# A decayed attention followed by a gated MLP on one core: bias placed in PSUM, decays moved to k, more transposes by DMA, and a new order of all engines

## The chip, the cores and the metric

The kernel runs on one core of one Trainium2 chip. The metric is the device time of one execution in microseconds (us). Engines are named as in the profile: PE is the matrix engine (PEld its weight load), DVE the vector engine, ACT the scalar engine, POOL the GpSimd engine, SP the engine whose queue issues most DMAs.

## The reference

Inputs are q, k and v of 4 batches, 8 heads, 768 tokens and 64 elements per head, and one decay per head. Attention has no softmax: a token attends to earlier tokens with a weight that decays with distance, and the reference computes it in blocks of 64 with a running state.

```
intra = einsum('bhic,bhjc->bhij', qb, kb) * Dmask      # lam ** (i - j) for i >= j
intra = einsum('bhij,bhjd->bhid', intra, vb)
inter = einsum('bhid,bhde->bhie', qb * lam_pow, kv_state)
kv_state = lam_block * kv_state + einsum('bhsd,bhse->bhde', kb * rev_pow, vb)
x = (intra + inter) as (batch, token, 512)
h = relu(x @ w_in)                        # 512 -> 1024
u, v = h[..., :512], h[..., 512:]
v_n = (v - mean(v)) / sqrt(var(v) + 1e-6)
v_s = einsum('ts,bsd->btd', w_spatial, v_n) + b_spatial[None, :, None]
out = (u * v_s) @ w_out                   # 512 -> 512
```

`w_spatial` is 768 x 768 and mixes tokens, so the second half of a batch can start only when all tokens of the batch have their normalised v.

## The kernel before, in words

**Steps and batches.** Work is cut into 12 steps of 256 tokens of all heads; steps 0 to 2 are batch 0, steps 3 to 5 batch 1, and so on. Within a step 256 tokens are two chunks of 128. Each partition holds two adjacent tokens, so a "row" of the DMA is 512 bytes.

**Names of the work.** Everything is written out by hand in one string, `ORDER`. A token such as `SC.5.1.2.T` is a function (`SC`, line 322), its numbers, and the engine whose queue it goes into: T is PE, D is DVE, A is ACT, P is POOL, S is SP. Each engine runs its own tokens in the order of the string; between engines only data dependences and buffers order them. So a token that waits holds up all later tokens of its engine.

For a step n:

- `LK`, `LQ`, `LV` (line 184) load 512 KB of k, q, v; 3 buffers each (`NIN`).
- `KC`, `QC` cast k and q to bf16. `VD` (line 292) multiplies v by the decay of its token and casts, on POOL. `QM` (line 277) multiplies q by its decay, `EQ` (line 313) does so on the transposed q.
- `TK`, `TQ` (line 300) transpose by 8 products with the identity on PE, and `EK`, `EQ` copy the result out of PSUM to `kT`, `qT`. For steps 8 to 11 `DK`, `DQ` (lines 283, 287) transpose by DMA from SP's queue instead.
- `SC` (line 329) makes scores, `MK` (line 333) masks them into `a_sb`; `KV` (line 345) adds to the state in PSUM bank 7, `SS` copies the state out; `AV` (lines 366, 375) makes the attention's output, `EX` copies it to `xT`.
- `PV` (line 401) and `PU` (line 439) are the two halves of `x @ w_in`; `EV`, `EU` (lines 406, 408) apply relu on the way out of PSUM. `BN`, `RA`, `RD`, `VN` (lines 416 to 430) normalise v.

For a batch: `PW.b.f.i` (line 461) is the product with `w_spatial`, 6 products of 384 columns; `GB` (line 466, DVE) adds the bias from PSUM to the f32 tile `vsb`; `GM` (line 472, mostly POOL) multiplies by u into `gT`; `PO` (line 478) is the last product, `EO` copies out, `ST` stores 256 KB. `WT` (line 451) transposes `w_spatial` once on PE. The two adjacent tokens of a partition make the token order of x differ from the natural one; `WT` and `GM` undo it with strided views.

```
    def g_b(e, bb, f, i, b):
        nc.vector.tensor_tensor(out=vsb[...], in0=bank(b)[:, 0:HW], in1=bsp[...], op=ALU.add)
    def g_m(e, bb, f, i):
        vec(e).tensor_tensor(out=gT[...] "p (a y m) -> p a y m", in0=vsb[...],
                             in1=uT[...] "p (a m y) -> p a y m", op=ALU.mult)
```

PSUM has 8 banks; banks 0 to 6 are handed out by the last numbers of the tokens, and a token that needs a bank waits for the last reader of it. `GT` (line 235) is a tiny POOL copy that reads a loaded tile; it stands before the weight loads `WI`, `WS`, `WO`, which POOL issues with a cast to bf16, so that these start after that tile has landed.

Of the kernel before, what the change touches and what calls it, by code (L numbers as in the profile page):

```python
# [16 lines left out]
LK.0.2.S lam.A msk.P LQ.0.2.S LK.1.2.S idn.P mkc.D LV.0.2.S LB.6.T pos.P LN.6.A LK.2.2.S LL.D KC.0.2.P LX.A  # L17
LQ.1.2.S TK.0.6.T LT.0.A QC.0.2.D LQ.2.2.S TQ.0.5.T EK.0.6.A EQ.0.5.D KC.1.2.A SC.0.0.0.T LV.1.2.S SC.0.1.2.T
LT.2.A MK.0.0.0.D TK.1.6.T VD.0.2.P EK.1.6.A MK.0.1.2.D LV.2.2.S LT.1.A AV.0.0.0.T LK.3.2.S KV.0.0.T SS.0.0.A
GT.1.1.P WI.0.P QC.1.2.D KV.0.1.T AV.0.1.0.T KC.2.2.A LQ.3.2.S GT.1.1.P WI.1.P TQ.1.6.T EX.0.1.1.A TK.2.5.T  # L20
EQ.1.6.D GT.1.2.P WS.1.P EX.0.0.0.A QC.2.2.D EK.2.5.A SC.1.0.2.T LQ.4.2.S GT.1.2.P WS.0.P SC.1.1.0.T
MK.1.0.2.D TQ.2.6.T SS.0.1.A VD.1.2.P EQ.2.6.D MK.1.1.0.D SC.2.0.2.T SC.2.1.4.T MK.2.0.2.D AV.1.0.0.T KV.1.0.T
LV.3.2.S MK.2.1.4.D SS.1.0.A KV.1.1.T VD.2.2.P AV.1.1.0.T SS.1.1.A PV.0.0.6.T EX.1.1.1.A EX.1.0.0.A PV.0.1.1.T
EV.0.0.6.A AV.2.0.2.T BN.0.0.D PV.1.1.6.T EV.0.1.1.D KV.2.0.T BN.0.1.D PV.1.0.5.T SS.2.0.A EV.1.1.6.D RA.0.A
AV.2.1.2.T BN.1.1.D PU.1.0.6.T BS.S EV.1.0.5.A RD.0.D PU.0.1.4.T VN.0.0.D EX.2.1.3.A KC.3.2.P BN.1.0.D
EX.2.0.2.A PU.1.1.5.T EU.0.1.4.A EU.1.0.6.D PV.2.0.3.T RA.1.A VN.0.1.D EU.1.1.5.A RD.1.D TK.3.6.T VN.1.1.D
EV.2.0.3.A PU.2.0.2.T VN.1.0.D EK.3.6.A BN.2.0.D PV.2.1.3.T EU.2.0.2.A PU.2.1.6.T EV.2.1.3.A LK.4.2.S WT.3.2.T
BN.2.1.D EU.2.1.6.A QC.3.2.P WT.4.3.T WT.0.5.T EW.3.2.D RA.2.A WT.1.6.T LK.5.2.S EW.4.3.D EW.0.5.A WT.5.4.T
WT.2.2.T RD.2.D VN.2.1.D EW.5.4.A TQ.3.3.T QC.4.2.P VN.2.0.D PU.0.0.5.T EW.2.2.A EQ.3.3.D LQ.6.2.S EW.1.6.A
TQ.4.4.T VD.3.2.P SC.3.1.0.T EU.0.0.5.A EQ.4.4.D SC.3.0.2.T PW.0.0.1.6.T LQ.5.2.S MK.3.1.0.D PW.0.1.1.5.T  # L30
GB.0.0.1.6.D LV.4.2.S MK.3.0.2.D PW.0.1.0.4.T GM.0.0.1.P KC.4.2.A PW.0.0.0.6.T GB.0.1.1.5.D GB.0.1.0.4.D
LK.6.2.S GM.0.1.1.P TK.4.5.T GB.0.0.0.6.D PW.0.2.1.4.T GM.0.1.0.P EK.4.5.D LK.7.2.S AV.3.0.0.T GT.0.5.P WO.P
GB.0.2.1.4.D SC.4.0.2.T SC.4.1.5.T KV.3.0.T MK.4.0.2.D PW.0.3.1.4.T GM.0.2.1.P SS.3.0.A LV.6.2.S QC.6.2.P
MK.4.1.5.D KV.3.1.T AV.3.1.0.T KC.5.2.A PW.0.3.0.3.T GM.0.0.0.P SS.3.1.D GB.0.3.1.4.D LV.5.2.S QC.5.2.A
TK.5.6.T EX.3.1.1.D GM.0.3.1.P PW.0.2.0.2.T GB.0.3.0.3.D EX.3.0.0.A VD.4.2.P EK.5.6.A GM.0.3.0.D TQ.5.3.T
GB.0.2.0.2.D PV.3.1.5.T EQ.5.3.D PU.3.0.6.T EV.3.1.5.A GM.0.2.0.P AV.4.0.0.T BN.3.1.D EU.3.0.6.A SC.5.1.2.T
SC.5.0.4.T LQ.8.2.S KV.4.0.T MK.5.1.2.D PV.3.0.6.T SS.4.0.A MK.5.0.4.D KV.4.1.T EV.3.0.6.A AV.4.1.0.T LK.8.2.S
KC.6.2.P PO.0.0.3.T EX.4.0.0.A BN.3.0.D EX.4.1.1.A PO.0.1.6.T EO.0.0.3.D RA.3.A LK.9.2.S PV.4.0.2.T RD.3.D
SS.4.1.D EO.0.1.6.A VN.3.1.D VD.6.2.P VN.3.0.D PV.4.1.3.T EV.4.0.2.A ST.0.0.S TK.6.6.T BN.4.0.D EV.4.1.3.A
PO.0.2.2.T EK.6.6.A BN.4.1.D VD.5.2.P TQ.6.3.T LV.9.2.S EO.0.2.2.A PU.3.1.5.T EQ.6.3.D RA.4.A PO.0.3.6.T  # L40
# [24 lines left out]
EU.9.0.6.A AV.10.1.0.T MK.11.1.4.D PW.2.0.1.3.T EX.10.1.1.A SS.10.1.D PW.2.2.0.6.T GM.2.3.0.D GB.2.0.1.3.D
AV.11.0.4.T EX.10.0.0.D GM.2.0.1.P GB.2.2.0.6.D KV.11.0.T PV.10.0.3.T SS.11.0.D GM.2.2.0.P VN.9.0.D
AV.11.1.4.T EV.10.0.3.A PW.2.2.1.6.T EX.11.1.5.A BN.10.0.D EX.11.0.4.A PO.2.1.5.T GB.2.2.1.6.D PO.2.2.4.T
GM.2.2.1.P EO.2.1.5.D PU.11.1.6.T ST.2.1.S EO.2.2.4.A PO.2.4.5.T ST.2.2.S EU.11.1.6.A PV.11.1.4.T PV.11.0.6.T
EV.11.1.4.A PV.10.1.3.T BN.11.1.D EV.11.0.6.A PO.2.3.2.T BN.11.0.D EV.10.1.3.A PU.11.0.6.T BN.10.1.D RA.11.A
EO.2.3.2.A PU.10.1.3.T RD.11.D RA.10.A ST.2.3.S VN.11.1.D EU.11.0.6.A RD.10.D VN.11.0.D PO.2.5.2.T EU.10.1.3.A  # L70
VN.10.0.D VN.10.1.D PU.10.0.6.T EO.2.5.2.A PW.3.1.1.3.T ST.2.5.S EU.10.0.6.D PO.2.0.2.T GB.3.1.1.3.D
PW.3.0.0.6.T GM.3.1.1.P EO.2.0.2.A ST.2.0.S PW.3.1.0.4.T GB.3.0.0.6.D GM.3.0.0.P PW.3.0.1.6.T GB.3.1.0.4.D
GM.3.1.0.P PW.3.2.0.4.T EO.2.4.5.A GB.3.0.1.6.D ST.2.4.S GM.3.0.1.D PW.3.3.0.6.T GB.3.2.0.4.D PW.3.2.1.5.T
GM.3.2.0.P GB.3.3.0.6.D GM.3.3.0.D PW.3.3.1.6.T GB.3.2.1.5.D PO.3.0.4.T GM.3.2.1.P GB.3.3.1.6.D PO.3.1.5.T
GM.3.3.1.P EO.3.0.4.A PO.3.2.6.T ST.3.0.S EO.3.1.5.A PO.3.3.4.T ST.3.1.S EO.3.2.6.A PO.3.4.5.T ST.3.2.S
EO.3.3.4.A PO.3.5.6.T ST.3.3.S EO.3.4.5.A ST.3.4.S EH.3.5.6.0.A EH.3.5.6.1.D SH.3.5.0.A SH.3.5.1.S
"""


@with_exitstack  # L80
def kernel(
    ctx: ExitStack,
    tc: tile.TileContext,
    q: bass.AP,
    k: bass.AP,
    v: bass.AP,
    lam: bass.AP,
    moe_w_in: bass.AP,
# [11 lines left out]
    NT = S // P  # L100
    NCH = DM // P
    NR = S // (2 * P)
    T2 = 2 * P
    Q64 = 64
    MID = S // 2
    NIN, NCA, NTR, NA, NX, NO, NVS = 3, 2, 2, 2, 3, 4, 2

    const = ctx.enter_context(tc.tile_pool(name="const", bufs=1))
    psum = ctx.enter_context(tc.tile_pool(name="psum", bufs=1, space=bass.MemoryType.PSUM))

    def sb(shape, dt, name):
        return const.tile(shape, dt, name=name)
# [422 lines left out]
```

## Time and profile before

| what | before |
|---|---|
| device time, median of 3 runs | 152.93 us (152.09 to 153.16) |
| span of the profiled execution, first to last instruction | 151.2 us |
| median less that span | 1.7 us |
| PE busy | 133.6 us, 88% of the span |
| DVE busy | 106.9 us, 71% |
| ACT busy | 81.4 us, 54% |
| POOL busy | 75.6 us, 50% |
| moved by DMA | 30.73 MB, 203 GB/s on average |

How to read it: all numbers of engines and of the trace are of one profiled execution, whose own record is the span; the time of a run is a little longer than its span, and the last rows of the table put the two side by side. Busy PE is not PE at its peak, since the ends of pipelined products are modelled: in the chain of waits eight 256-column products stand at 0.87 us, while one of them alone is listed with 273 ns. Below, "row" is a group of instructions of one line and shape, "slice" is one fortieth of the span (3.78 us), and the DMA share is the mean busy share of the 16 DMA engines (it reaches 1.4 in places).

### The profile page before, as it was taken

Reading aid. Unit: us, or ns where it says so; the run is one execution under the profiler, and the core shown is the slowest. Engines: PE = TensorE matmul, PEld = TensorE weight load, DVE = VectorE, ACT = ScalarE, POOL = GpSimd, SP = SyncE. Lnnn points to the kernel's source line nnn. Section 1 sums busy time; section 2 is a strip of 40 time slices with the busy share of each in tenths; the row PEclk is TensorE's granted clock in tenths of the full one; section 3 lists DMA queues with packets and bytes.
Section 4 is the critical chain, followed back from the end, with each engine's and each line's share of the span. In section 5 each row is a group of like instructions: output and inputs, shape, how many; then the busy total and the mean of one; then the engine's idle time right before and its main releaser. Section 6 shows DMA issues by size and latency. Waiting matters only on the chain.

```text
span 151.2 us, 4756 instructions
## 1 busy us (share of the span) xinstructions
PE 133.6 (88%) x2026; PEld 87.2 (58%) x2026; DVE 106.9 (71%) x190; ACT 81.4 (54%) x146; POOL 75.6 (50%) x74
## 2 busy tenths in 40 slices
PE   1274947999999989977999999999999999999990
PEld 1264844677766754645766756556657655666540
DVE  1454593986999998685747799999958981936701
ACT  3987815698623837737724434765553344831161
POOL 7425980203669922780039975990293240016520
PEclk9999999999999999999999999999999999999999
DMA  3999999999988998999999799994170003121255
GB/s 108 300 290 290 283 216 216 217 248 304 281 221 237 172 301 216 269 310 342 319 341 276 142 306 311 202 208 177 41 138 4 2 4 139 57 81 72 74 219 197
DMA packets 52040, 30.73 MB, mean 203 GB/s; under 512 B 9522, under 2 KB 48946, under 8 KB 52018
## 3 DMA queue, kind: packets, MB, share of 16 engines
q1 hardware_dynamic: 49488, 27.53, 71.0%
q0 software_dynamic: 2384, 2.75, 10.6%
q8 instruction: 16, 0.26, 0.7%
q10 hardware_dynamic: 146, 0.13, 0.3%
q14 instruction: 6, 0.05, 0.1%
HBM read 24.77 MB, written 6.29 MB: 205 GB/s over the span
## 4 chain that ended last, share of the span: by engine, by line
PE 70%; DMA 16%; DVE 5%; SPq 4%; issue 2%; POOL 0%; ACT 0%; ACTq 0%
PE ps L461 20%; PE ps L439 13%; PE ps L401 13%; PE ps L478 11%; DMA q_in<-in_q_dram 10%; DMA win_sb<-in_moe_w_in_dram 6%; SPq L184 4%; PE ps L375 3%; PE ps L345 3%; PE ps L329 3%; PE ps L300 2%; PE ps L366 2%; PE ps L451 1%; DVE vsb L466 1%; DVE vn L430 1%
## 5 line engine op out<-in xcount | busy, mean ns | idle before, releaser
L472 POOL TENSOR_TENSOR gT<-vsb,uT 128x384 bf16<-128x384 f32 x27 | 30.1, 1128 | 33.6 <-DVE vsb L466 33.3
L461 PE MATMUL ps<-wt_sb,vn 128*128 128x384 bf16 x192 | 33.9, 327 | 0.0
L292 POOL TENSOR_TENSOR vd<-v_in,lv 128x1024 bf16<-128x1024 f32 x12 | 22.8, 1905 | 17.1 <-issue 6.4
L333 DVE TENSOR_TENSOR a_sb<-ps,m 128x1024 bf16<-128x1024 f32 x24 | 28.4, 1214 | 1.8 <-PE ps L329 1.6
L416 DVE BATCH_NORM_STATS2 st<-vh 128x6 f32<-128x512 bf16 x24 | 16.5, 688 | 11.9 <-ACT vh L406 11.7
L461 PEld LDWEIGHTS <-vn 128*128 128x128 bf16 x192 | 17.9, 98 | 11.9
L401 PE MATMUL ps<-win_sb,xT 128*128 128x512 bf16 x96 | 23.6, 380 | 0.8 <-DMA win_sb<-in_moe_w_in_dram 0.8
L439 PE MATMUL ps<-xT,win_sb 128*128 128x256 bf16 x192 | 24.1, 273 | 0.0
L478 PE MATMUL ps<-wout_sb,gT 128*128 128x512 bf16 x96 | 23.4, 380 | 0.0
L466 DVE TENSOR_TENSOR vsb<-ps,bsp 128x384 f32<-128x384 f32 x32 | 17.6, 552 | 6.8 <-PE ps L461 5.4
L439 PEld LDWEIGHTS <-win_sb 128*128 128x128 bf16 x192 | 18.3, 98 | 4.4
L168 ACT ACTIVATE o_sb<-ps 128x512 f32<-128x512 f32 (+1 forms) x21 | 12.3, 586 | 14.9 <-PE ps L478 10.7
L406 ACT ACTIVATE vh<-ps 128x512 bf16<-128x512 f32 x21 | 12.5, 597 | 13.6 <-PE ps L401 13.6
L406 ACT ACTIVATE uT<-ps 128x512 bf16<-128x512 f32 x22 | 13.2, 598 | 6.9 <-PE ps L439 6.7
L401 PEld LDWEIGHTS <-xT 128*128 128x128 bf16 x96 | 8.8, 98 | 9.6 <-issue 0.8
L478 PEld LDWEIGHTS <-gT 128*128 128x128 bf16 x96 | 9.0, 98 | 8.8
L168 ACT ACTIVATE s_sb<-ps 128x256 bf16<-128x256 f32 x14 | 5.3, 381 | 16.1 <-PE ps L345 16.1
L430 DVE TENSOR_SCALAR vn<-vh,mv,rstd 128x512 bf16<-128x512 bf16 x24 | 12.5, 551 | 0.3
L375 PE MATMUL ps<-a_sb,vd 64*64 64x128 bf16 x384 | 11.1, 225 | 1.7 <-DVE a_sb L333 1.0
L168 ACT ACTIVATE kc<-k_in 128x1024 bf16<-128x1024 f32 x7 | 7.4, 1056 | 8.4 <-PE ps L345 5.1
L168 ACT ACTIVATE xT<-ps 128x512 bf16<-128x512 f32 x19 | 10.5, 591 | 1.4 <-PE ps L375 1.3
L329 PE MATMUL ps<-qT,kT 64*64 64x128 bf16 x384 | 8.4, 233 | 2.5 <-DVE qT L313 2.5
(64 smaller groups left out, 155.6 us busy)
## 6 DMA issues: line engine op xcount, KB each, us to landing
k_in<-in_k_dram SPq DMA_DIRECT2D x12, 512.0 KB, 7.3
q_in<-in_q_dram SPq DMA_DIRECT2D x12, 512.0 KB, 7.3
v_in<-in_v_dram SPq DMA_DIRECT2D x12, 512.0 KB, 7.1
out_dram<-o_sb SPq DMA_DIRECT2D x23, 256.0 KB, 2.5
wsp_raw<-in_moe_w_spatial_dram POOLq DMA_DIRECT2D x2, 576.0 KB, 16.1
win_sb<-in_moe_w_in_dram POOLq DMA_DIRECT2D x2, 512.0 KB, 10.6
wout_sb<-in_moe_w_out_dram POOLq DMA_DIRECT2D x1, 512.0 KB, 10.7
bsp<-in_moe_b_spatial_dram SPq DMA_DIRECT2D x1, 384.0 KB, 8.1
```

Of the source, the lines that this page charges most:

```text
L168: nc.scalar.activation(out=o, in_=i, func=AF.Copy)
L292: vec(e).tensor_tensor(out=vd[n % NCA][:, h], in0=v_in[n % NIN][:, h], in1=lv[:, n % NR, h].unsqueeze(3).broadcast_to((P, h.stop - h.start ...
L333: nc.vector.tensor_tensor(out=a_sb[n % NA][:, i].rearrange("p o w j x -> p (o w) (j x)"), in0=bank(b, 2).rearrange("p o (w y) -> p (o w) y ...
L375: nc.tensor.matmul(out=po[row(w), c ^ o, c, i], lhsT=vd[n % NCA][row(c), 4 * o + u, j, :], rhs=a[row(c), i, o, w, j, :], start=(r == 0 and ...
L401: nc.tensor.matmul(out=bank(b), lhsT=x[:, c, g], rhs=win_sb[:, g, DH:DFF], start=(g == 0), stop=(g == NCH - 1))
L406: nc.scalar.activation(out=o, in_=i, func=AF.Relu)
L416: nc.vector.bn_stats(out=st6[p2][:, t], in_=vh[p2][:, t])
L439: nc.tensor.matmul(out=pu[:, f2].rearrange("p (c x) -> p c x", c=2), lhsT=win_sb[:, g, f * P:(f + 1) * P], rhs=x[:, :, g, :], start=(g == ...
L461: nc.tensor.matmul(out=bank(b)[:, 0:HW], lhsT=vn[bb % 2][:, s, f * P:(f + 1) * P], rhs=wt_sb[:, s, i * HW:(i + 1) * HW], start=(s == 0), s ...
L466: nc.vector.tensor_tensor(out=vsb[(bb * 4 + f) % NVS][:, i * HW:(i + 1) * HW], in0=bank(b)[:, 0:HW], in1=bsp[:, i * HW:(i + 1) * HW], op=A ...
L472: vec(e).tensor_tensor(out=gT[bb % 2][:, f, cols].rearrange("p (a y m) -> p a y m", m=2, y=Q64), in0=vsb[(bb * 4 + f) % NVS][:, cols].rear ...
L478: nc.tensor.matmul(out=bank(b), lhsT=gT[bb % 2][:, f, t * P:(t + 1) * P], rhs=wout_sb[:, f, :], start=(f == 0), stop=(f == NCH - 1))
```

## The change

- **Bias.** `GB` is gone. A new `GP` copies the bias of 384 tokens into the PSUM bank ahead of `PW` (25 on ACT, 7 on DVE), `PW` adds to it (no product of the group starts the bank anew), and `GM` reads PSUM, now all 32 on DVE. So that the bank adds, `SC` and `PU` start a bank once and not per part.
- **Decays on k.** `VD` becomes a plain cast `VC` (10 on POOL, 2 on ACT); k gets the decay in `KM`, in two halves of 512 columns (20 on POOL, 4 on DVE) in place of 12 casts of 1024.
- **Transposes.** Steps 5 to 11 use `DK`, `DQ` (14 DMA transposes, before 8); steps 0 to 4 use PE (before 0 to 7). Steps 0, 1 and the k of step 2 are transposed, cast and copied in halves. `QM` works in halves too: 13 on POOL, 1 on DVE (before 6 and 2).
- **Natural order.** `EX` writes `xT` with the two tokens of a partition interleaved, so `GM` and `WT` (36 products in place of 72) have plain views.
- **Order.** All six queues are ordered anew. There are 12 output buffers instead of 4; the first store stands behind 28 loads in SP's queue, where before it stood behind 25. The first loads are k0, k1, q1, q0, q2, v0, v1, k2, v2; before k0, q0, k1, v0, k2, q1, q2, v1, v2. Tile 5 of batch 3, which ended the kernel with its two halves copied and stored apart on two queues, is now made in two halves (`PH`) earlier, and the kernel ends with the whole tile 2 (`EO`, `ST`).
- **Products of ones.** `FL` issues 28 products of 128x256 of a constant tile into unused columns of bank 7, in six places ahead of PE's first waits.

The numbers of the other moves: on DVE `EX` 5 to 7, `EV` 3 to 7, `EU` 2 to 7, `EO` 3 to 6, `SS` 6 to 4, `EW` 2 to 3; what DVE takes ACT loses.

```diff
-LK.0.2.S lam.A msk.P LQ.0.2.S LK.1.2.S idn.P mkc.D LV.0.2.S LB.6.T pos.P LN.6.A LK.2.2.S LL.D KC.0.2.P LX.A
...
+one.D LK.0.S lam.A msk.P mkc.D FL.6.256.1.T LB.0.T LN.0.A posk.P LL.D LX.A KM.0.0.D LK.1.S KM.0.1.D LQ.1.S idn.P
+FL.16.256.0.T TK.0.1.1.T EK.0.1.1.D pos.P LT.1.A LT.2.A LT.0.A KM.1.0.P FL.2.256.0.T TK.1.0.2.T EK.1.0.2.D
+TK.0.0.3.T KM.1.1.P QC.1.0.P TK.1.1.4.T TQ.1.0.5.T EQ.1.0.5.D QC.1.1.P TQ.1.1.6.T EQ.1.1.6.D EK.0.0.3.A
+EK.1.1.4.A LQ.0.S QC.0.1.P QC.0.0.D FL.1.256.0.T TQ.0.1.0.T EQ.0.1.0.D TQ.0.0.1.T EQ.0.0.1.D LQ.2.S QC.2.1.P
+GT.0.1.P WI.0.P SC.1.1.2.5.T MK.1.1.2.5.D GT.1.2.P WI.1.P SC.0.0.3.6.T TQ.2.1.4.T MK.0.0.3.6.D QC.2.0.A
...
-    NIN, NCA, NTR, NA, NX, NO, NVS = 3, 2, 2, 2, 3, 4, 2
+    HW = S // 2
+    NIN, NCA, NTR, NA, NX, NO = 3, 2, 2, 2, 3, 12
...
+    def c_ones(e):
+        nc.vector.memset(ones, 1.0)
+
+    def f_l(e, k, w, new):
+        for i in range(k):
+            nc.tensor.matmul(out=bank(SB)[:, T2:T2 + w], lhsT=ones[:, 0:P], rhs=ones[:, 0:w],
+                             start=(new == 1 and i == 0), stop=True, skip_group_check=True)
...
+    def decay(e, dst, src, ln, n, x):
+        u = part(x)
+        vec(e).tensor_tensor(
+            out=dst[n % NCA][:, u].rearrange("p u m o d -> p o (u m) d"),
+            in0=src[n % NIN].rearrange("p (o u) m d -> p o u m d", o=2)[:, :, u].rearrange("p o u m d -> p o (u m) d"),
+            in1=ln[:, n % NR].rearrange("p (o u) m -> p o u m", o=2)[:, :, u].rearrange("p o u m -> p o (u m)")
+            .unsqueeze(3).broadcast_to((P, 2, 2 * (u.stop - u.start), D)), op=ALU.mult)
+
+    def k_m(e, n, x):
+        decay(e, kc, k_in, lv, n, x)
...
-    def v_d(e, n, x):
-        h = slice(*hx(x))
-        vec(e).tensor_tensor(out=vd[n % NCA][:, h], in0=v_in[n % NIN][:, h],
-                             in1=lv[:, n % NR, h].unsqueeze(3).broadcast_to((P, h.stop - h.start, 2, D)), op=ALU.mult)
+    def v_c(e, n):
+        copy(e, vb[n % NCA].rearrange("p h m d -> p (h m d)"), v_in[n % NIN].rearrange("p h m d -> p (h m d)"))
...
     def e_x(e, n, z, b):
...
+        copy(e, xT[n % NX][:, z::2].rearrange("p k (y m) -> p k m y", m=2),
+             bank(b).rearrange("p (k m y) -> p k m y", k=NCH, m=2))
...
         for a in range(NT):
-            for m in range(2):
-                nc.tensor.transpose(out=pw[row(m), a * P:(a + 1) * P], in_=wsp_raw[:, a, s * P + m:(s + 1) * P:2],
-                                    identity=ident)
+            nc.tensor.transpose(out=pw[:, a * P:(a + 1) * P], in_=wsp_raw[:, a, s * P:(s + 1) * P], identity=ident)
...
+    def g_p(e, bb, f, i, b):
+        copy(e, bank(b)[:, 0:HW], bsp[:, i * HW:(i + 1) * HW])
+
     def p_w(e, bb, f, i, b):
-        HW = S // 2
         for s in range(NT):
             nc.tensor.matmul(out=bank(b)[:, 0:HW], lhsT=vn[bb % 2][:, s, f * P:(f + 1) * P],
-                             rhs=wt_sb[:, s, i * HW:(i + 1) * HW], start=(s == 0), stop=(s == NT - 1))
-
-    def g_b(e, bb, f, i, b):
-        HW = S // 2
-        nc.vector.tensor_tensor(out=vsb[(bb * 4 + f) % NVS][:, i * HW:(i + 1) * HW], in0=bank(b)[:, 0:HW],
-                                in1=bsp[:, i * HW:(i + 1) * HW], op=ALU.add)
-
-    def g_m(e, bb, f, i):
-        HW = S // 2
+                             rhs=wt_sb[:, s, i * HW:(i + 1) * HW], start=False, stop=(s == NT - 1),
+                             skip_group_check=True)
+
+    def g_m(e, bb, f, i, b):
         cols = slice(i * HW, (i + 1) * HW)
-        vec(e).tensor_tensor(out=gT[bb % 2][:, f, cols].rearrange("p (a y m) -> p a y m", m=2, y=Q64),
-                             in0=vsb[(bb * 4 + f) % NVS][:, cols].rearrange("p (a y m) -> p a y m", m=2, y=Q64),
-                             in1=uT[bb % 2][:, f, cols].rearrange("p (a m y) -> p a y m", m=2, y=Q64), op=ALU.mult)
+        nc.vector.tensor_tensor(out=gT[bb % 2][:, f, cols], in0=bank(b)[:, 0:HW], in1=uT[bb % 2][:, f, cols],
+                                op=ALU.mult)
```

The parts of the new order that the prediction speaks of, as they stand in it (each token with its engine letter; the pieces are not adjacent):

```
... QC.2.1.P GT.0.1.P WI.0.P ... GT.1.2.P WI.1.P ... VC.0.P ... GT.0.1.P WS.0.P ... VC.1.P ... GT.2.1.P WS.1.P
... WT.4.0.T WT.0.6.T EW.0.6.D EW.4.0.D WT.1.5.T EW.1.5.D WT.2.1.T EW.2.1.A ... GP.0.2.1.2.D ... PW.0.2.1.2.T ...
... LV.4.S ... DQ.5.S ... DK.5.S ... LV.5.S ... LQ.6.S ... LK.6.S LV.6.S ... LQ.7.S LV.7.S LK.7.S ... DQ.6.S DK.6.S
... EU.11.0.3.D EU.10.0.2.D GM.3.1.1.5.D ... PO.3.0.3.T EO.3.0.3.A ST.3.0.S PO.3.2.5.T EO.3.2.5.A ST.3.2.S
```

## The prediction

> **What bounds the kernel now.** I read four views in this order: busy time by slice, chain of waits, groups, then the timelines of single engines.
>
> ```profile
> PE 133.6 (88%) x2026; PEld 87.2 (58%) x2026; DVE 106.9 (71%) x190; ACT 81.4 (54%) x146; POOL 75.6 (50%) x74
> ...
> PE   1274947999999989977999999999999999999990
> ...
> DMA  3999999999988998999999799994170003121255
> ...
> PE 70%; DMA 16%; DVE 5%; SPq 4%; issue 2%; POOL 0%; ACT 0%; ACTq 0%
> ```
>
> The reader is to see three stages. Slices 1 to 6 (to 23 us): PE is short of data and DMA full. Slices 7 to 18 (to 69 us): PE nearly full with dents, DMA still full. From there to the end PE is full. In order of time the chain runs
>
> ```profile
> 6.65 7.30 DMA q_in<-in_q_dram
> 13.95 0.05 issue
> 14.00 0.65 POOL seen L235
> 14.65 9.29 DMA win_sb<-in_moe_w_in_dram
> 23.94 0.04 issue
> 23.98 1.89 PE ps L401 x8
> ...
> 57.49 7.18 DMA q_in<-in_q_dram
> 64.67 0.02 issue
> 64.69 0.88 DVE qc L277
> ```
>
> so the start is k and q, then `w_in`, which waits at POOL until q1 has landed; and near 64 us DVE stands behind a `QM` that waits for q8 (1.45 us idle). From 68.85 to 147.5 us PE has no idle time.
>
> The true work of PE I count from the chain's back-to-back pieces: 8 transposes 0.45, `SC` 0.22, `AV` 0.46, `KV` 0.24, `PV`, `PU` and `PO` 0.87, `PW` 0.97 to 1.0 us. With the counts of the order this is 16 x 0.45 + 24 x 0.225 + 24 x 0.46 + 20 x 0.24 + 72 x 0.87 + 32 x 1.0 + 2.13 (`WT`) = about **125 us**. Of the 151.2, some 26 are thus not work: 17.8 before the first `PV` at 24 us (6.2 us of work is done by then), about 3.6 between 40.3 and 68.85 (24.9 of work in 28.5), 3.7 at the end, the rest small.
>
> **The change part by part**, against the span of 151.2 us; the median of the runs, 152.93, lies 1.7 above it, and I add that 1.7 at the end.
>
> *PE's work.* Steps 5, 6, 7 lose `TK` and `TQ`: 6 x 0.45 = 2.7. `WT`: 36 whole transposes at 0.45/8 = 2.0 in place of 2.13. `PH` is 8 products of 256 columns, 0.87, as `PO`. `PW`, `SC` keep their count. Together **-2.8**, if PE is the bound where they stood; nothing where it is not.
>
> *Start.* The first loads landed, by who waited for them, at 4.9 (first), 6.75, 8.55, 10.45 (fourth) and 13.95 us (sixth), 1.8 us apart. `WI` now stands behind `QC.2.1` on POOL, which needs q2, the fifth load: 12.2. POOL before it: `KM.1` in two halves from 6.75 at 1.05 each (row of L277 on POOL, median 1048 ns), four half casts of 0.52 (L172, 1.04 whole), each behind its load; `QC.2.1` ends at 12.75, `WI` goes at 13.0 instead of 14.65 and with the same 9.3 us lands at 22.3. By then PE's own chain (steps 0 and 1 whole, `SC.2.1`) is done at about 21.8, counting `KM.2` from 19. So PV could start 1.7 earlier. But the two `WS` loads have `VC.0`, `VC.1` (1.04 each) and the landing of v1 ahead of them: the second goes at about 18.2, not 17.43. They took 14.7 and 17.5 us to land, so 32.9 to 35.7; PE reaches `WT` after 10.9 us of `PV`, `PU`, `AV` and `KV`, at 33.2. There up to 2.5 us of the lead are waited away. I take **-1.2**, ends +1 and -1.7.
>
> *Products of ones.* The first three sets of 8 transposes took 1.03 us each up to 17.6 us; the one at 18.47 took 0.62, with a granted clock of 1.00 throughout. The 28 products run in waits; the set of 16, at twice a slow transpose, is 16 x 0.24 = 3.9 us after 3.5 and ends at 7.4, where `KM.0` ends at 7.2. Loss at most 0.5, gain at most 0.6 (one transposed set), both before the wait for `w_in` that hides them: 0. If that wait shrinks, the gain shows. The Trainium skill ("TensorE: Matmul & The Clock Gate", What's actually happening) says the clock is halved until some 3.4 us of sustained work and again after an idle window as long; by it 16 products would warm PE and the following waits would cool it, so the sum would stay as it is.
>
> *Middle, 40 to 69 us.* The 3.6 us of lost time had three causes in view: a `GM` on DVE, `QM` waiting for q8, and DVE's `VN` and `MK` behind it. The first two are gone from these places. Against that DVE gains work.
>
> ```profile
> L466 DVE TENSOR_TENSOR vsb<-ps,bsp 128x384 f32<-128x384 f32 x32 | 17.6, 552 | 6.8 <-PE ps L461 5.4
> ```
>
> and, from the answers for single lines (shortest, median and longest in ns),
>
> ```profile
> L472 DVE TENSOR_TENSOR gT<-vsb,uT x5: 551/828/2675, 50.6 to 141.1; 128x384 bf16<-128x384 f32 x5
> L430 DVE TENSOR_SCALAR vn<-vh,mv,rstd x24: 394/407/1178, 30.0 to 132.0; 128x512 bf16<-128x512 bf16 x24
> ```
>
> Its 32 `GM` from PSUM take the price of the 32 `GB` (0.55, the same shape): 0. Gone: 5 `GM` 6.1, `QC`, `KC`, `QM` about 4.2, `EQ` 2.1, `SS` 0.8. New: `GP` 7 x 0.5, `KM` 4 x 0.83, `EV`, `EU`, `EX`, `EO` 14 x 0.67 = 9.4, `EK` 2.0, `EW` and the constant 0.7. Net +5.7: 112.6 us busy. Between 22 and 68 us I add up the new DVE order at 41.5 (overlap taken off) to 44.5 us in 46: as full as PE. `GP` on ACT is 0.49 by the rows of 256 and 512 columns (0.38, 0.59), 25 x 0.49 = 12.3; ACT drops 20 for casts, copies and relus, so it stays at 73. POOL loses `GM` 30.1, `VD` 22.8 and `KC` 4.2 and gains 20 `KM`, 7 `QM` (1.05) and 10 `VC` (1.04): 58. I take **-1.5**; ends -3.6 (all stalls go) and +6.6 (rival B).
>
> The spread of 551 to 2675 and 394 to 1178 ns is one operation at unequal moments: the 2675 one runs while POOL does a `VD`. The Trainium skill ("SBUF — State Buffer", SBUF: two separate sides) says DVE and POOL share a port pair as an exclusive lock, for DVE operations with two SBUF inputs or in a two-port mode, not with one input in PSUM. By it `GM` from PSUM never pays, and DVE would shed the 3.3 us by which its five `GM` exceed 5 x 0.55; the sum above has these 3.3 inside the 6.1.
>
> *DMA.* Six more transposes. Those before landed in 3.1 to 4.0 us from issue. In 80 to 84 us, with two of them, the bytes fell from 340 to 220 GB/s: 0.48 MB, 0.7 us each; at 1.6 us, what SP's issue of one takes, is the other end. 4 to 10 us of DMA time, beside a share that falls to 0.56 and below after 104 us. v11, loaded from 88.9 on, is used at 108.7. So 0, unless waits add up. On SP, `DQ.5` waits for `AV.3.1` and holds `LV.5` and six more loads; but 17 loads and the weights (12 MB, 250 GB/s) keep DMA busy until about 50, and `AV.3.1` ends 23.5 us of PE's work after 22.3, near 47 with small losses.
>
> *New waits after 69 us.* Before there were none on PE. `GP` waits for its bank and `PW` for `GP` (0.49), and behind a late `GP` stand ACT's relus; 26 us of PE's work follow `SC.11`, so PE asks for its transposes near 115; q11 and k11 stand on SP behind `DQ.10`, which needs `AV.8.1`, and if they go at 101 to 104 and land 6 later, two `QM` and two `KM` on POOL (4.2) and 3.6 to landing give 115 to 118. **+0.5**, ends 0 and +3.
>
> *End.* The last copy is whole, 0.60 instead of 0.39, and its store 2.5 instead of 1.75 to landing: **+0.9**, ends 0.2 and 1.4.
>
> *Sum.* -2.8 - 1.2 - 1.5 + 0.5 + 0.9 = -4.1: span 147.1, time **148.8 us**. The far ends give -7.9 (145.0).
>
> **Rivals.** *A, all goes well*: DVE keeps up and no stall is left; -2.8 - 1.7 - 3.0 + 0.7 = -6.8, time 146.1 (145 to 146.5). For it: QM's and GM's places on DVE are cleared. Against: DVE's sum above.
>
> *B, slower: DVE becomes the bound from 22 to 68 us.* Its 44.5 us plus the 7.8 us that it stood idle in 22 to 69 before (busy 39.2 of 47, waits for ACT and PE that stay) make 74.6, not 68: +6.6 on 147.1 is 153.7, time **155.4**. With the lower sum of 41.5 it is 152.4. From some 7 us of idle DVE in that stretch the gain of 4.1 is gone (22.3 + 43 + 7 = 72.3, against 68 planned). For it: DVE was 97% busy in 40 to 60 us. Against: much of the old idle was waiting for ACT's relu (11.7 us over the run), which DVE now partly does itself.
>
> *C, the DMA queue's own waits*: SP stands for `AV` at `DQ.5`, `DQ.6`, `DQ.8`, and loads of steps 8 to 11 come late by more than the slack of 2 to 6 us; 6 us of lost DMA time, half of it covered, gives back 3 to 4: 152 to 153, no change.
>
> **How the numbers follow.** A measurement here can tell about 1% from no change (1.5 us). Forecast (146.5 to 151.4) 0.50, A 0.17, C and the mild half of B (151.4 to 154.5) 0.14, the full B and worse 0.19. Faster 0.67, same 0.14, slower 0.19. Range: 145.0, the far end of A, to 155.5, B; some 0.15 lies outside, mostly above.
>
> **What would show it.** PE near 122 us of chain pieces and its first `PV` at 22 to 23; `WT` waiting for `wsp_raw` about a microsecond; `gT` on DVE at 0.55 in all 32; 12 to 14 us of `bsp` copies on ACT; DVE at 110 to 115 busy, 95% in 25 to 65 us; transposes landing in 3 to 4 us. Wrong would be: `DQ.5` landing after 55 us, PE waits for `kT` or `qT` beyond 2 us each, `PW` waiting for `GP`, or PE idle by more than 3 us after 70.

## The result, and the profile after

| what | before | after |
|---|---|---|
| device time, median | 152.51 us (152.05 to 153.16, 4 runs) | 171.53 us (170.94 to 172.47, 4 runs) |
| span of the profiled execution | 151.2 us | 169.1 us |
| PE, DVE, ACT, POOL busy | 133.6, 106.9, 81.4, 75.6 us | 142.8, 112.4, 74.9, 56.3 us |

The changed kernel takes 1.126 times as long (95% interval 1.120 to 1.133). Faster was forecast, and the time lies far above the range. Some executions of a kernel fall into a slower state, so medians below are of all executions, and ratios and their intervals compare only those outside that state.

The page of the changed kernel, busy time, slices and shares of the chain:

```profile
PE 142.8 (84%) x1974; PEld 88.3 (52%) x1974; DVE 112.4 (66%) x210; ACT 74.9 (44%) x148; POOL 56.3 (33%) x70
...
PE   6765879899997991999956995999699968999991
...
PEclk9998555999999999699999998799999999999999
...
PE 68%; DVE 17%; DMA 4%; ACT 4%; issue 2%; SPq 1%; POOL 0%; DVEq 0%
```

Before, PE was nearly full from slice 8 on (0.7 or more in each). Now its row has dents all the way (the 1 in slice 16, the 5 in slice 21; a slice is now 4.23 us), and the granted clock is halved in slices 5 to 7 and lowered in slices 17, 25 and 26. DVE's share of the chain has risen from 5% to 17%.

The chain of waits, its start (start, length in us):

```profile
3.25 7.11 DMA q_in<-in_q_dram
...
12.35 1.17 DVE a_sb L352
13.55 0.42 PE ps L347 x16
```

`win_sb` is gone from it: the early weight loads do what they were to do. `a_sb`, the mask `MK`, has come in (10% of the whole chain). The costs of single instructions are as forecast (groups of instructions: count, busy us, mean ns, idle before and who ended it):

```profile
L352 DVE TENSOR_TENSOR a_sb<-ps,m 128x1024 bf16<-128x1024 f32 x24 | 29.1, 1218 | 7.3 <-PE ps L347 3.4
...
L173 ACT ACTIVATE ps<-bsp 128x384 f32<-128x384 f32 x25 | 12.0, 491 | 12.2 <-DVE a_sb L352 8.4
```

Before, the mask's row was

```profile
L333 DVE TENSOR_TENSOR a_sb<-ps,m 128x1024 bf16<-128x1024 f32 x24 | 28.4, 1214 | 1.8 <-PE ps L329 1.6
```

The mask takes 1218 ns, 1214 before. It isn't slower; others wait for it. PE's waits for it, first in the kernel before and then in the changed kernel (us in total, times, longest):

```profile
PE ps L300 <- DVE a_sb L333: 1.2, 1, 1.2
PE ps L375 <- DVE a_sb L333: 1.0, 1, 1.0
...
PE ps L366 <- DVE a_sb L333: 0.5, 1, 0.5
```

```profile
PE ps L347 <- DVE a_sb L352: 7.9, 6, 1.6
PE ps L488 <- DVE a_sb L352: 5.9, 2, 3.8
PE ps L477 <- DVE a_sb L352: 1.8, 1, 1.8
...
PE ps L416 <- DVE a_sb L352: 0.4, 1, 0.4
```

That is 16.0 us of PE waiting for the mask; before it was 2.7. L347 is `SC`, L488 `PO`, L477 `PW`, L416 `PV`: products that have nothing to do with the mask's result. ACT waits for it too, 8.4 us in its bias copies (the row above). One place of the timeline shows how:

```profile
63.99 0.75 ACT L173 ACTIVATE xT<-ps 128x512 bf16<-128x512 f32 x1
...
64.77 2.36 DVE L352 TENSOR_TENSOR a_sb<-ps,m 128x1024 bf16<-128x1024 f32 x2 [2.75 <-ACT xT L173]
...
67.18 3.56 PE L488 MATMUL ps<-wout_sb,gT 128*128 128x512 bf16 x8 [3.83 <-DVE a_sb L352]
```

By the order this is `EX.4.0.2` on ACT (it reads bank 2), then `MK.5.1.1.4` and `MK.5.0.0.6` on DVE (banks 1 and 4, banks 0 and 6), then `PO.0.5.3` on PE (bank 3). The first mask waits 2.75 us for a reader of bank **2**, and the product into bank **3** waits until the second mask has ended. Neither bank belongs to a mask; both lie between its two. The code that does it is in the diff's lines of `SC` and `MK`, which the excerpt above leaves out:

```diff
     def m_k(...):
         nc.vector.tensor_tensor(
-            out=a_sb[n % NA][:, i].rearrange("p o w j x -> p (o w) (j x)"),
-            in0=bank(b, 2).rearrange("p o (w y) -> p (o w) y", w=2),
+            out=a_sb[n % NA][:, i].rearrange("p o w j x -> p o w (j x)"),
+            in0=ps[:, b0:b1 + 1:b1 - b0].rearrange("p o (w y) -> p o w y", w=2),
```

Before, the two banks of a score pair were always neighbours. Now they are any two, and one instruction reads both by a view that steps from `b0` to `b1`. 18 of the 24 pairs are apart; together they step over 45 banks (0 and 6, three times, over five). **Theory 1**: the order kept between instructions takes such a view for the whole range, so each mask waits for, and holds up, all banks between. (Which layer between the kernel's text and the chip keeps this order, no run shows.) **Rivals**: the grain of the mask (one instruction of 1.2 us instead of two of 0.7 lets go of its banks late), the products of ones, the longer DVE work, the bias preset.

### The profile page after: what moved, and what is told of

Same layout as the page of the kernel before. It is cut to its first block, busy times and chain, and to the rows that moved or that the text cites. A ratio compares the mean times of both kernels' runs of the same rounds, so it can differ in the third digit from the quotient of the medians.

```text
span 169.1 us, 4639 instructions
## 1 busy us (share of the span) xinstructions
PE 142.8 (84%) x1974; PEld 88.3 (52%) x1974; DVE 112.4 (66%) x210; ACT 74.9 (44%) x148; POOL 56.3 (33%) x70
## 3 DMA queue, kind: packets, MB, share of 16 engines
q0 software_dynamic: 2384, 2.75, 9.4%
## 4 chain that ended last, share of the span: by engine, by line
PE 68%; DVE 17%; DMA 4%; ACT 4%; issue 2%; SPq 1%; POOL 0%; DVEq 0%
PE ps L477 18%; PE ps L488 13%; PE ps L416 12%; DVE a_sb L352 10%; PE ps L454 10%; DMA q_in<-in_q_dram 4%; PE ps L394 3%; PE ps L347 3%; PE ps L364 3%; PE ps L316 3%; PE ps L385 2%; DVE vn L445 2%; DVE gT L483 1%; SPq L188 1%; ACT xT L173 1%
## 5 line engine op out<-in xcount | busy, mean ns | idle before, releaser
L477 PE MATMUL ps<-wt_sb,vn 128*128 128x384 bf16 x192 | 33.9, 326 | 1.9 <-DVE a_sb L352 1.8
L352 DVE TENSOR_TENSOR a_sb<-ps,m 128x1024 bf16<-128x1024 f32 x24 | 29.1, 1218 | 7.3 <-PE ps L347 3.4
L286 POOL TENSOR_TENSOR kc<-k_in,lv 128x512 bf16<-128x512 f32 x20 | 20.5, 1043 | 37.0 <-PE ps L364 16.8
L488 PE MATMUL ps<-wout_sb,gT 128*128 128x512 bf16 x92 | 24.3, 401 | 5.9 <-DVE a_sb L352 5.9
L416 PE MATMUL ps<-win_sb,xT 128*128 128x512 bf16 x96 | 27.2, 424 | 1.4 <-ACT xT L173 0.7
L477 PEld LDWEIGHTS <-vn 128*128 128x128 bf16 x192 | 17.9, 98 | 14.0 <-issue 2.0
L483 DVE TENSOR_TENSOR gT<-ps,uT 128x384 bf16<-128x384 f32 x32 | 16.9, 551 | 8.4 <-PE ps L477 7.6
L454 PEld LDWEIGHTS <-win_sb 128*128 128x128 bf16 x192 | 18.2, 98 | 4.2 <-issue 0.2
L286 POOL TENSOR_TENSOR qc<-q_in,lqn 128x512 bf16<-128x512 f32 x13 | 13.5, 1052 | 14.1 <-DMA q_in<-in_q_dram 7.8
L347 PE MATMUL ps<-qT,kT 64*64 64x128 bf16 x384 | 10.4, 227 | 8.4 <-DVE a_sb L352 7.9
L173 ACT ACTIVATE ps<-bsp 128x384 f32<-128x384 f32 x25 | 12.0, 491 | 12.2 <-DVE a_sb L352 8.4
L488 PEld LDWEIGHTS <-gT 128*128 128x128 bf16 x92 | 8.9, 102 | 15.5 <-DVE a_sb L352 4.0
L416 PEld LDWEIGHTS <-xT 128*128 128x128 bf16 x96 | 9.6, 106 | 14.1 <-issue 4.4
L177 POOL CAST vb<-v_in 128x1024 bf16<-128x1024 f32 x10 | 10.4, 1045 | 18.9 <-DMA v_in<-in_v_dram 18.9
L421 ACT ACTIVATE vh<-ps 128x512 bf16<-128x512 f32 x17 | 10.0, 596 | 13.5 <-PE ps L416 7.3
L347 PEld LDWEIGHTS <-kT 64*64 64x64 bf16 x384 | 7.2, 110 | 12.3 <-issue 10.7
L421 ACT ACTIVATE uT<-ps 128x512 bf16<-128x512 f32 x17 | 9.8, 591 | 4.9 <-PE ps L454 4.8
```

The lines of the kernel that those rows point to most:

```text
L173: nc.scalar.activation(out=o, in_=i, func=AF.Copy)
L177: nc.gpsimd.tensor_copy(out=o, in_=i)
L286: vec(e).tensor_tensor(out=dst[n % NCA][:, u].rearrange("p u m o d -> p o (u m) d"), in0=src[n % NIN].rearrange("p (o u) m d -> p o u m d" ...
L347: nc.tensor.matmul(out=pa[o][row(c), w, j], lhsT=kT[n % NTR][row(o), u, j, c * Q64:(c + 1) * Q64], rhs=qv(n, o, u, c), start=(w == 0 and j ...
L352: nc.vector.tensor_tensor(out=a_sb[n % NA][:, i].rearrange("p o w j x -> p o w (j x)"), in0=ps[:, b0:b1 + 1:b1 - b0].rearrange("p o (w y) ...
L416: nc.tensor.matmul(out=bank(b), lhsT=x[:, slot(c, g)], rhs=win_sb[:, g, DH:DFF], start=(g == 0), stop=(g == NCH - 1))
```

## The experiments

### The mask per bank, and the products of ones

Three kernels of one chip, whose kernel before had 151.88 us. The first makes each mask two instructions of one bank:

```diff
-        nc.vector.tensor_tensor(out=a_sb[...], in0=ps[:, b0:b1 + 1:b1 - b0]..., ...)
+        for o, b in ((0, b0), (1, b1)):
+            nc.vector.tensor_tensor(out=a_sb[n % NA][:, i, o]..., in0=bank(b)..., ...)
```

> The changed kernel with each mask product MK written as two DVE instructions, one per PSUM bank, in place of one over a view that steps from bank b0 to bank b1; the same numbers are computed. Theory 1 (bank range): the one instruction is ordered against every access to the banks that lie between b0 and b1, so PE, ACT and DVE stand for each other without need; in the changed kernel PE's idle time that ends with DVE's a_sb is 16.0 us (7.9, 5.9, 1.8, 0.4) and ACT's 17.6. With the split most of it goes: span 169.1 falls by 9 to 16, time 155 to 162, although DVE gets 24 more instructions (about 0.1 us each). Theory 2 (clock): the half clock from 16 to 29 us is the main loss; it stays, time 168 to 172. Theory 3 (SP's queue): SP stands from 41.8 to 52.9, 67.7, 81 to 92.4 us and data comes late; time 167 to 172.

Measured: 152.08 us (151.63 to 153.86), 1.003 times before (0.999 to 1.008). The whole loss is gone, more than the 9 to 16 us that theory 1 had been given. Its page, and the longest of its waits of PE:

```profile
PE 138.5 (91%) x1974; PEld 86.5 (57%) x1974; DVE 114.6 (75%) x234; ACT 75.1 (49%) x148; POOL 57.1 (38%) x70
...
PEclk9999955799999999999999999999999999999999
```

```profile
PE ps L264 <- DVE ones L260: 1.5, 1, 1.5
PE ps L467 <- DVE wt_sb L175: 1.4, 1, 1.4
PE ps L478 <- DVE vn L446: 1.2, 2, 0.6
PE ps L395 <- DVE a_sb L353: 1.1, 1, 1.1
```

16.0 us of waits for the mask have become 1.1, though DVE is busier by 2.2 us (114.6 for 112.4) and the bias is still preset; so neither DVE's load nor the preset is the loss. But the forecast's gain isn't there either; that is followed further down.

The second is the changed kernel without the products of ones, the third the first and the second together:

```diff
-one.D LK.0.S lam.A msk.P mkc.D FL.6.256.1.T LB.0.T ...
+one.D LK.0.S lam.A msk.P mkc.D LB.0.T ...
```

> The changed kernel without the 28 products of ones. Theory 2 (clock): the products warm PE from about 6 us on, the waits at 12 to 15.6 us cool it, and it runs at a granted clock of 0.50 from 16 to 29 us, through the first 13 products of PV (0.43 instead of 0.215 us each, 2.8 us) and the attention before them. Without them PE is slow at first, as in the kernel before, and at full speed by about 20 us: the time falls by 2.5 to 4.5, to 166.5 to 168.5. Theories 1 and 3: the start is set by data and by the waits for MK, so the time stays within 1 us of 171.

> Both: MK per bank, and no products of ones. Theory 1 with 2: the gains of the two runs add, time 151 to 158. Theory 1 alone: as the split alone within 1 us. Theory 3: 165 to 171.

Measured: 173.71 us (172.26 to 174.87, ratio 1.139, 1.127 to 1.152), and 153.87 us (151.33 to 156.56, ratio 1.007, 1.001 to 1.014). The ones are no cause of the loss. Nor can their own worth be told from nothing: with the mask split the ratio is 1.003 with them and 1.007 without, about 0.6 us, and the two intervals overlap. (The medians, which are of all executions, lie 1.8 us apart.)

### Two instructions, but over both banks

The control for the grain: as many instructions and the same sizes as in the first run, but each still spans both banks.

```diff
-        for o, b in ((0, b0), (1, b1)):
+        for w in range(2):
-                in0=bank(b).rearrange("p (w y) -> p w y", w=2),
+                in0=ps[:, b0:b1 + 1:b1 - b0, w * 2 * P:(w + 1) * 2 * P],
```

> A control for the split: MK again as two DVE instructions of 128x512, but cut the other way, so that each still steps from bank b0 to bank b1. DVE has the same 48 mask products as with the split by bank. Theory 1 (bank range): the range between the banks is covered as before, so the loss stays: 170 to 176. Rival (grain): the split helped because shorter instructions free banks and DVE earlier; then the time falls as with the split by bank, 151 to 156.

Measured: 174.87 us (174.27 to 176.09); before, on this chip, 152.83; ratio 1.148 (1.138 to 1.157). Its waits of PE are those of the changed kernel:

```profile
PE ps L347 <- DVE a_sb L353: 8.0, 6, 1.6
PE ps L489 <- DVE a_sb L353: 6.1, 2, 4.0
PE ps L478 <- DVE a_sb L353: 1.9, 1, 1.9
```

So neither the number nor the size of the masks brings the loss, only that their view spans banks. The grain falls.

### The same view in the kernel before

The reverse: nothing of the change but the view. The kernel before gets its banks renumbered so that score pairs lie apart (20 of the 24 masks, over 57 banks), and the stepping mask; `SC` and `AV` address the renumbered banks one by one. The control has the same banks and a mask per bank.

```diff
+    PB = (0, 4, 1, 5, 2, 3, 6, 7)
-    def bank(b, n=1):
-        return ps[:, b] if n == 1 else ps[:, b:b + n]
+    def bank(b):
+        return ps[:, PB[b]]
-            in0=bank(b, 2).rearrange("p o (w y) -> p (o w) y", w=2),
+            in0=ps[:, b0:b1 + 1:b1 - b0].rearrange("p o (w y) -> p o w y", w=2),
```

> The kernel before with one thing changed: its seven banks are renumbered, so that the two banks of a score pair lie apart (bank 0 with 4, 1 with 5, 3 with 6; one pair stays adjacent), and MK reads them by one stepping view as in the changed kernel. 20 of its 24 masks then span 57 banks that they do not use (the changed kernel: 18 and 45). Order, engines and all sizes stay. Theory 1 (a stepping view makes the mask wait for, and hold up, all banks between): the loss appears in the kernel before too, 158 to 172 us, ratio 1.03 to 1.12, with new waits of PE and ACT for a_sb; DVE's busy time stays at 107. Rival (the view only hurts together with the new order, or not at all): 152 to 154 us.

> The control to the run before it: the same renumbered banks in the kernel before, but MK as two instructions of one bank each. Theory 1: 152 to 155 us (24 more DVE instructions, some 3 us of DVE work, partly hidden), PE's waits for a_sb as in the kernel before. Rival (the renumbering itself costs): as long as the run before it.

Measured, with 153.12 us for the kernel before: 167.33 us (165.46 to 167.63), ratio 1.093 (1.086 to 1.101), and the control 152.55 us (152.09 to 153.86), ratio 1.006 (1.002 to 1.010). The waits of PE with the stepping mask:

```profile
PE ps L464 <- DVE a_sb L336: 3.7, 4, 1.3
...
PE ps L442 <- DVE a_sb L336: 2.4, 1, 2.4
PE ps L331 <- DVE a_sb L336: 2.3, 1, 2.3
PE ps L369 <- DVE a_sb L336: 1.7, 2, 1.3
PE ps L481 <- DVE a_sb L336: 1.7, 1, 1.7
PE ps L404 <- DVE a_sb L336: 1.1, 1, 1.1
```

12.9 us, against 2.7 in the kernel before; the control has none for the mask among its listed waits. The view alone, in another kernel with another order, costs 14 us. With the split that takes the loss away, theory 1 is shown from both sides.

### Where the forecast's gain went

With the mask per bank the median is 152.08 us, and 148.8 was forecast: 3.3 us are missing. (The profiled execution of the split kernel is the longest of its ten, 153.86 us; its span of 152.1 us lies 5.0 above the span of the forecast.) Five runs look for them, all with the mask per bank.

`EX` without interleaving the two tokens of a partition:

```diff
-        copy(e, xT[n % NX][:, z::2].rearrange("p k (y m) -> p k m y", m=2),
-             bank(b).rearrange("p (k m y) -> p k m y", k=NCH, m=2))
+        copy(e, xT[n % NX][:, z::2], bank(b).rearrange("p (k y) -> p k y", k=NCH))
```

> MK per bank, and EX copies the attention's output to xT in the order in which it stands in PSUM, without interleaving the two tokens of a partition; the tokens of x are thus permuted and the output is not the reference's. ACT's EX took 743 ns with the interleaving write and 591 in the kernel before. Theory (price of the interleaving write): the copies fall to 0.59 us, 17 x 0.15 = 2.6 us less on ACT; ACT is 49% busy, so the time falls by 0 to 1.5 from 152.1. Rival (free): nothing but the row changes, within 0.5.

Measured: 152.2 us (150.25 to 155.15), ratio 0.992 (0.987 to 0.998), where the split kernel has 1.003 (0.999 to 1.008) on another chip. The rows of this copy on ACT, with interleaving (the changed kernel) and without (this run):

```profile
L173 ACT ACTIVATE xT<-ps 128x512 bf16<-128x512 f32 x17 | 11.8, 744 | 8.0 <-PE ps L394 5.0 <-DVE a_sb L352 2.9
```

```profile
L173 ACT ACTIVATE xT<-ps 128x512 bf16<-128x512 f32 x17 | 9.5, 596 | 4.7 <-PE ps L395 4.7
```

The interleaved write costs 0.15 us each, 2.3 us of ACT and 0.3 of DVE. Of the time it costs about 1%, by two ratios from two chips; theory and rival lie too close together to be told apart by them.

More products of ones, since the clock of the split kernel is halved from about 19 to 28 us (its row of PEclk above):

```diff
-... MK.1.0.2.5.D LV.0.S VC.0.P FL.2.256.0.T
+... MK.1.0.2.5.D LV.0.S VC.0.P FL.20.256.0.T
 (and 6 and 4 more ahead of two later waits)
```

> MK per bank, with 20 products of ones in place of 2 ahead of AV.0.0 and 6 and 4 new ones ahead of AV.1.0 and SC.2.1, where PE waits. Theory 2b (clock): PE falls to a granted clock of 0.50 at about 18 us because of the wait from 13.5 to 16 us; kept busy, it stays at 1.00, PV's first 16 products take 0.22 instead of 0.43 us each and the attention before them half, so the time falls by 2 to 4 from 152.1, to 148 to 150. Rival (data): the start is set by the transposes of k2 and by w_in, and DVE holds PE up to 43 us; the time stays within 1 us, or rises by up to 1.

Measured: 153.15 us (150.42 to 154.41), too wide a spread for an interval; no gain shows, and none is excluded. PE's first `PV` in the timeline of the split kernel and then of this run:

```profile
24.20 1.91 PE L417 MATMUL ps<-win_sb,xT 128*128 128x512 bf16 x4
```

```profile
23.96 1.03 PE L417 MATMUL ps<-win_sb,xT 128*128 128x512 bf16 x4
```

The clock stays whole, four products take 1.03 instead of 1.91 us, and the first `PW` starts at 41.36 instead of 43.30 us. Of this lead of 1.9 us 0.6 is left at PE's last product (147.8 against 148.4 us). On the way stand three waits of PE, 2.7 us together, which the split kernel doesn't have; the timeline of this run:

```profile
74.74 0.64 PE L347 MATMUL ps<-qT,kT 64*64 64x128 bf16 x32 [0.23 <-DMA kT<-kc]
79.85 0.64 PE L347 MATMUL ps<-qT,kT 64*64 64x128 bf16 x32 [0.85 <-DMA kT<-kc]
90.66 0.42 PE L347 MATMUL ps<-qT,kT 64*64 64x128 bf16 x16 [1.57 <-DMA kT<-kc]
```

These are the DMA transposes of k for steps 6, 7 and 8. So in the run made last, k of steps 7 and 8 goes back to PE:

```diff
-EX.5.0.1.D DK.7.S PV.4.1.6.T
+EX.5.0.1.D PV.4.1.6.T
-PW.1.2.0.2.T AV.6.0.1.3.T
+PW.1.2.0.2.T TK.7.2.0.T EK.7.2.0.D AV.6.0.1.3.T
 (and the same for step 8)
```

> The kernel of e6 (MK per bank, 20, 6 and 4 more products of ones) with k of steps 7 and 8 transposed on PE again (8 products and one DVE copy each) in place of the transposes by DMA. In e6 PE stood first at the preset product of batch 0 1.9 us ahead of e1, and then waited 0.85 and 1.57 us for these two transposed k between 75 and 91 us. Theory (the transposes by DMA, priced at nothing in the prediction, take the lead back): these two waits go, PE gains 2.4 us and pays 0.9 us of products, so the span is 1 to 2 us under e6's 151.6 and the time 150 to 152 us. Rival (the lead would be lost to the next wait anyway): 152 to 154 us, with new waits of PE of 1.5 us or more behind 69 us.

Measured: 155.59 us (154.44 to 156.26), ratio 1.021 (1.015 to 1.026). The waits for transposed k are gone, as the theory had it, but the time lies above both ranges, and the longest wait of PE behind 69 us is 1.06 us, where the rival had new ones of 1.5 or more. So neither holds, and why this kernel is slower is not shown. The first `PW` came later too, at 42.24 us for 41.36, ahead of any place that differs from the run with more ones; the listed waits of PE between 31 and 131 us are now nearly all for DVE, which is busy for 117.4 us (two of them; the first is `PW` waiting for `GP`, as the prediction's list feared):

```profile
42.24 2.11 PE L478 MATMUL ps<-wt_sb,vn 128*128 128x384 bf16 x12 [0.39 <-DVE ps L175]
73.39 3.59 PE L478 MATMUL ps<-wt_sb,vn 128*128 128x384 bf16 x21 [1.06 <-DVE vn L446]
```

Relief for DVE was tried twice: ten copies and relus of batches 0 and 1 moved to ACT, and then six of these (the expectation says seven) together with the added products of ones and an earlier `RA.3` on ACT.

```diff
-... PV.2.0.2.T EU.1.1.5.D EU.1.0.1.A EV.2.0.2.D ...
+... PV.2.0.2.T EU.1.1.5.A EU.1.0.1.A EV.2.0.2.A ...
```

> MK per bank, with ten copies and relus of batches 0 and 1 moved from DVE to ACT (EX.2.1, EU.1.1, EV.2.0, EW.0, EW.4, GP.0.2.1, EV.4.0, EX.5.0, EU.4.1, EU.4.0; 6.5 us by their rows). Theory (DVE is the bound in 31 to 43 and 63 to 75 us, the prediction's rival B): PE's wait for wt_sb (1.4) and vn (1.2) goes and the time falls by 1 to 3.5, to 148.5 to 151. Rival (order, not load): what is late is ACT's RA and the chain through it, and moving work to ACT delays these; the time stays within 1 us or rises by up to 2.

> The changed kernel with MK per bank, more products of ones (20, 6 and 4 ahead of three waits) and seven copies and relus of batches 0 and 1 moved from DVE to ACT, with batch 1's statistics (RA.3) put ahead on ACT. If both the slow clock of the start and the tie of DVE and ACT in 31 to 44 us hold the split kernel back, this gives 149.5 to 151.5 us; if relief of either engine only moves the wait to the other, as the two runs with one of these steps alone showed, 152 to 154 us.

Measured: 153.69 us (150.76 to 156.27, ratio 0.997, 0.987 to 1.007), and 152.4 us (150.81 to 155.33, ratio 1.002, 0.997 to 1.007). In the first, PE's wait for `wt_sb`, now copied by ACT, falls from 1.4 to 0.6 us, but its wait for `vn` grows from 1.2 to 1.8 us, which fits the rival of that run. In the second DVE is busy for 109.7 us, 4.9 less than in the split kernel, and ACT for 77.9; PE now waits for ACT's copies of `wt_sb` (0.35 and 0.21 us) where it had waited for DVE's. No version that computes the reference's output beats the kernel before by what a measurement can tell.

### The bias by an addition again

Mask per bank, no `GP`; `GB` on DVE adds the bias into four f32 tiles, `GM` on POOL multiplies.

```diff
-                             ... start=False, stop=(s == NT - 1),
+                             ... start=(s == 0), stop=(s == NT - 1),
+    def g_b(e, bb, f, i, b):
+        nc.vector.tensor_tensor(out=vsb[...], in0=bank(b)[:, 0:HW], in1=bsp[...], op=ALU.add)
```

> The changed kernel with MK per bank and the preset of the bias undone: no GP; PW opens its bank; GB on DVE adds the bias into four f32 tiles, and GM on POOL multiplies by u, all in natural token order. ACT loses about 12 us, DVE some 3.5, POOL gains about 35 us. If the preset is worth something on the path (theory: PW no longer waits for GP, but GM waits for POOL): 152 to 156 us; if ACT's relief in 31 to 44 us weighs more: 150 to 152 us.

Measured: 168.12 us (166.66 to 170.57), ratio 1.101 (1.091 to 1.111), far outside both expectations. POOL is busy for 85.1 us, and its `GM` stand between the `KM` and `QM` that the order put there. It waits in front of them for DVE's additions, and PE waits for POOL (all waits, us in total, times, longest):

```profile
POOL gT L484 <- DVE vsb L479: 30.6, 9, 17.7
...
PE ps L489 <- POOL gT L484: 8.0, 3, 4.1
```

In this order the preset can't be taken out alone: POOL's queue stands still where its steps wait for `PW`. What the preset would be worth in an order made for the addition was not tried.

## Why the prediction was wrong

**The step that failed** is the one on waits: "New waits after 69 us ... **+0.5**, ends 0 and +3", and beside it the middle, with ends of -3.6 and +6.6. The new waits that they price are those for `GP`, for DVE's load and for the transposes; `MK` stands in them only as work of DVE that comes late, and its new view in no term, though it was in the diff. The sum of DVE's work leaves the mask at its price (1214 ns), which held (1218), and doesn't ask which banks the one instruction now touches. After 69 us PE is idle for 9.2 us (to 147 us), and over the whole run it waits 16.0 us for the mask. The view cost 17.0 us of the span (169.1, against 152.1 with the mask per bank): 14.9 are PE's waits for the mask (16.0 less 1.1). The other 2.1 were not taken apart; the halved clock is large enough for them, for by the mean granted clock (0.939 and 0.964) it lasts about 21 us in the changed kernel and 11 in the split one. An estimate could have been had from the rows of before: 18 masks over other banks, each of 1.21 us, make 22 us if each holds PE for its own length. With that the range would have reached to about 170.

None of the three rivals was this. The list of what would make it wrong had the sign ("PE idle by more than 3 us after 70"), but not the cause.

Step by step, from the changed kernel and the split one:

- *Prices of operations*: right. `GM` from PSUM 551 ns (524 to 559 over all 32, where the five on DVE from SBUF had 551 to 2675), the bias copies 491 ns and 12.0 us of ACT, DVE 112.4 us (112.6 forecast), ACT 74.9 (73), POOL 56.3 (58).
- *Start*, -1.2: the times of issue were right, the gain wasn't there. `WI` goes at 13.07 us (13.0 forecast) and the second `WS` at 17.84 (18.2) in the split kernel, and neither `win_sb` nor `wsp_raw` ends a listed wait of PE. But the faster of the two loads of `w_in` takes 10.1 us to land, where 9.3 was taken over, so that no part of it is there before 23.2 us; and PE's own chain, forecast to end at 21.8, reaches the first `PV` at 24.20 (24.96 in the changed kernel). The halved clock, by which 16 products take 0.64 us instead of 0.42 from 16 us on (changed) or 19 us on (split), is not all of it: at the full clock, with more products of ones, the first `PV` is still at 23.96, though those products take time of PE's own.
- *Products of ones*, 0: no run tells their worth from 0, but the reasoning missed a cost. They do not keep the clock: in the split kernel the last of them ends at 14.9 us, a stretch with gaps follows, and the clock is 0.50 from about 19 to 28 us, with `PV` in it (from 16 to 29 us in the changed kernel). I had read the Trainium skill's rule on the clock ("TensorE: Matmul & The Clock Gate", What's actually happening) as leaving the sum as it was; the rows of this case are against that reading, as the slow stretch took in the first products of `PV`, which run back to back, and came without an idle stretch of the length that the rule names. A row was misread too: before, not the first three but all five sets of 8 transposes up to 17.5 us took 1.03 to 1.06 us. The granted clock stands at 1.00 there, so that row does not show the slow start.
- *Middle*, -1.5: about right in sign once the mask is split. PE is idle for 1.6 us between 31 and 69 us, 2.6 before. The stretch that rival B feared did not come: from 22 to 68 us DVE is busy for 38.3 us in the split kernel, as before (38.2), where 41.5 to 44.5 were added up. Yet DVE is the engine that PE waits for there.
- *Transposes by DMA*, 0: right for the changed and the split kernel, where none of PE's listed waits is for them. `DQ.5` goes at 52.85 us in the changed kernel, and as no transpose of q lands in under 3.2 us it lands after 55; the prediction took that for a sign of being wrong, but `SC.5` runs only at 62.1. They are next in line, though: with PE 1.9 us earlier it waits 2.7 us for them.
- *End*, +0.9: wrong. From PE's last product to the end of the span it takes 3.7 us in all three kernels (147.5 to 151.2, 165.4 to 169.1, 148.4 to 152.1).
- *PE's work*, -2.8: no run isolates it. PE's busy time can't show it, since the products of ones and the slow products count in it.

In the profiled execution of the split kernel PE ends at 148.4 us, where the forecast has 142.5. Of these 5.9 us the first `PV` is 1.4 late (24.2, where -1.2 on 24.0 gives 22.8), and the halved clock under `PV` costs some 1.9 (16 products of the first `PV`s in 1.91 + 3.74 us, against 1.03 + 2.76 at the full clock). PE's idle time behind that is 3.1 us, most of it for DVE's `wt_sb` (1.4) and `vn` (1.2), where the forecast itself leaves 2.6 (3.6 less 1.5, and 0.5): 0.5 more. Some 2 us stay unaccounted for; this execution is 1.8 us above the median of its kernel. The parts are not shown to be separable: each relief that was tried (clock, DVE's load, transposed k) shortened a wait and brought up or lengthened another. What holds the split kernel at 152 us is thus left open beyond this: DVE, ACT and the transposes by DMA each turned up as the next wait.

## What to carry to other kernels

When an instruction's view changes, ask not only how long it runs but what it touches in the eyes of whatever orders the instructions: a view that steps over banks or tiles may count as all that lies between, in both directions. The mask's length times the number of such views gives the size of the loss (here 22 us, with 17 measured, and 24 us for the kernel before with 14 measured). It is no bound, for the instruction also waits itself (2.75 us in the place shown). In a trace the sign is a wait for a result that the waiting instruction doesn't use, in a bank that the releasing one doesn't own; one instruction per bank, at 2 us more DVE work, removed it here. And where PE is full within a few per cent, as here, relieving one engine may give nothing back: none of the five runs that tried came out more than 1% under the kernel before. So forecast such a gain as zero until the next two waits have been priced.

## What the runs showed of the hardware that was not expected

- In the changed kernel a gap of 3.8 us in PE's work is paid twice. In its busy time by stretch (the two stretches from 63.4 us; PE, PEld, DVE, ACT, POOL, granted clock, DMA share, GB/s) the clock after it is 0.51, and the eight products of `PO` take 3.56 us, 1.74 at the full clock:

```profile
63.40:67.10 3.70, 0.00 (x0) 0.00 (x0) 2.33 (x2) 1.33 (x3) 2.22 (x3) 1.00 0.91 250
67.10:70.60 3.50, 3.42 (x8) 1.04 (x8) 0.02 (x1) 0.00 (x0) 3.50 (x5) 0.51 1.09 287
```

- No such gap is needed. In the split kernel PE is busy for 2.30 of the 4 us before 18 us, with no wait above 1.13 us, and from about 19 us the clock is halved; with more products of ones it is busy for 3.56 of these 4 us and keeps its clock. But the kernel before is busy for 3.30 of 6 us between 18 and 24 us and keeps it too, so that a share of busy time alone doesn't decide it. What does is open.
- An interleaved bf16 write costs ACT 744 ns for 128x512 elements, a plain one 596 ns; on DVE it is 723 and 679 ns.
- POOL's product from two SBUF tiles takes 913 ns in natural token order (128x384, in the run with the added bias) and 1128 ns with the permuted views of the kernel before.
